# Linear attention, one core: shared wait registers, a warm-up of nine wide matmuls, and VectorE's first head in another order

## The chip, the cores and the metric

The kernel runs on one core of a Trainium2 chip. The metric is the device time of one execution in microseconds (us). TensorE (PE) multiplies, VectorE (DVE), ScalarE (ACT) and GpSimd (POOL) do the elementwise work, SyncE (SP) issues the transfers.

## The reference

For each of 32 heads, q, k and v are 2048 x 128 in bf16:

```python
phi_q = jnp.where(q > 0, q + 1, jnp.exp(q)) + 1e-6
phi_k = jnp.where(k > 0, k + 1, jnp.exp(k)) + 1e-6
kv = jnp.einsum("bhsd,bhse->bhde", phi_k, v)
z = jnp.einsum("bhsd->bhd", phi_k)
num = jnp.einsum("bhqd,bhde->bhqe", phi_q, kv)
den = jnp.einsum("bhqd,bhd->bhq", phi_q, z)[..., None] + 1e-6
return num / den
```

Inputs are 50.3 MB, the output is 16.8 MB.

## The kernel before

phi(x) is computed as min(exp(x), 1) + 1e-6 plus max(x, 0), and the two summands are kept apart: for k they are `emk_sb` and `rk_sb`, for q `emq_sb` and `rq_sb`. A product with phi is then two matmuls into the same PSUM place.

One head goes through these steps. SP loads k, v and q (L371 to L373, 512 KB each) into one of six buffers each. ACT takes exp of k (`ek_sb`, L376). POOL takes max(k, 0) (`rk_sb`, L379; for head 1 DVE does it), DVE min(exp, 1) + 1e-6 (`emk_sb`, L382). For five of the sixteen tiles of 128 rows (`ADD`) POOL adds the two (L387). PE transposes q in two halves of eight tiles (L415, into `xT_ps`) and builds kv (L397) and, where no column of ones beside v does it, z with a one-column matmul (L330, the helper `mm_held`, which uses the weights that are loaded already). ACT and DVE copy kv and z out (`kvs_sb`, L406, L408). ACT takes exp of the transposed q (L426); relu of q is done by DVE for the first half (L435) and by ACT for the second (L433), for heads 0 and 1 by DVE for both. DVE makes `emq_sb` (L447). PE multiplies phi(q) with kv and z (L463, L464, into `o_ps`: five banks of three tiles, the sixteenth tile shared between the first two), DVE adds 1e-6 to the denominators, takes reciprocals and multiplies (L485, L491, L496, L503), and SP stores 512 KB (L549).

The order on each engine is written out by hand: every operation is added to a `Plan` with a key, and the operations of an engine are issued in the order of their keys. `place` (L350) overrides keys for the first heads. `Plan.emit` works out which semaphore values each operation has to wait for, and leaves out waits that earlier ones imply.

PE's stream of heads 1 to 30 is a hardware loop of five turns of six heads (`run_loop`, L165). Since a semaphore's awaited value grows from turn to turn, it stands in a register. Each semaphore x has a register of its own, set by `reg_mov` just ahead of the loop (L180); each wait is followed by a `reg_add` to the next awaited value (L188, L189):

```python
eng.wait_ge(sem_of(x), reg[x])
eng.reg_add(reg[x], reg[x], (l[i + 1] if i + 1 < len(l) else l[0] + step[x]) - v)
```

Ahead of head 0 PE runs a warm-up on zeros (`warm`, L340): 42 matmuls of 125 columns, the first with a load of weights (L344), the others through `mm_held`. They write columns of three `o_ps` banks that no result uses.

PE's order around the start is: warm-up, transposes of head 0, kv of head 0, the register moves, and the loop with transposes and kv of head 1, numerators of head 0, transposes and kv of head 2, and so on. The transposes of head 1 overwrite `xT_ps` and wait, half by half, for exp and relu of head 0; kv of head 1 waits for the copies of head 0 (L406, L408).

DVE's order for the first head is: emk of head 0, relu of the first half, rk of head 1, relu of the second half, emq of head 0, z of head 0, emk of head 1.

SP's order of loads at the start is k, q, v of head 0, k, q, v of head 1, k and q of head 2, k of head 3, v of head 2, and so on. Stores come late: the store of head h has the key h + 1 + 0.18 h, so that loads go ahead of them and a line of stores is left at the end.

Of the kernel before, what the change touches and what calls it, by code (L numbers as in the profile page):

```python
# [12 lines left out]
def _ap(base: bass.AP, elem_offset: int, dims):  # L13
    return bass.AP(base.tensor, base.offset + elem_offset, [list(base.ap[0])] + [list(d) for d in dims])
# [6 lines left out]
class Plan:  # L21
# [3 lines left out]

    def __init__(self):
        self.ops = []
        self.writer = {}
        self.readers = {}

# [31 lines left out]
    def emit(self, nc, block, sems, dma_sem, loop):  # L62
        order = self.order()
# [4 lines left out]
        ops = order["pe"]  # L68
        l0, l1 = (next(x for x in range(len(ops)) if ops[x].tag == t) for t in loop[:2])
        n = (l1 - l0) // loop[2]  # L70
# [26 lines left out]
        at = {e: 0 for e in order}  # L97
        left = sum(len(l) for l in order.values())
        waits = {}
        while left:  # L100
            moved = False
            for e, ops in order.items():
                while at[e] < len(ops):
                    op = ops[at[e]]
# [3 lines left out]
                    k = known[e]  # L108
# [22 lines left out]
        def sem_of(s):  # L131
            return dma_sem(s[1:]) if s[0] == "dma" else sems[s[0]]

        def emit_op(e, eng, op):
            last = op.emit(eng)
            if op.dma:
                last.then_inc(dma_sem(op.dma), 16)
            elif op.sem is not None:
                last.then_inc(sems[op.kind], 1)

        def turns_of(ops, l0, n, turns):
            body = []
            for i in range(n):
                same = [ops[l0 + t * n + i] for t in range(turns)]
                assert len({o.sem is None for o in same}) == 1
                asked = [dict(waits[id(o)]) for o in same]
                for t, o in enumerate(same):
                    for s in {s for a in asked for s in a}:
                        full = max([d.val for d in o.deps if d.sem == s and not (d.eng == "pe")], default=None)
                        if full is not None:  # L150
                            asked[t][s] = full
                for s in asked[1]:
                    if s not in asked[0]:
                        asked[0][s] = 2 * asked[1][s] - asked[2][s]
                        assert 0 < asked[0][s] <= ops[l0 - 1].clock.get(s, 0), (s, asked)
                assert len({tuple(sorted(a)) for a in asked}) == 1, asked
                row = []
                for s in asked[0]:
                    steps = {asked[t + 1][s] - asked[t][s] for t in range(turns - 1)}
                    assert len(steps) == 1, (s, asked)  # L160
                    row.append((s, asked[0][s], steps.pop()))
                body.append((same[0], row))
            return body

        def run_loop(e, eng, l0, n, turns):  # L165
            body = turns_of(order[e], l0, n, turns)
            seq, step, plan = {}, {}, []
            for _, row in body:
                for x, v, d in row:
                    assert step.setdefault(x, d) == d  # L170
                    seq.setdefault(x, []).append(v)
            for x, l in seq.items():
                before = max(l) - step[x]
                if 0 < before and order[e][l0 - 1].clock.get(x, 0) < before:
                    eng.wait_ge(sem_of(x), before)
                seq[x] = sorted({v for v in l if v > before})
            reg = {}
            for k, (x, l) in enumerate(seq.items()):
                reg[x] = eng.alloc_register(f"turn_{k}")
                eng.reg_mov(reg[x], l[0])  # L180
            at = {x: 0 for x in seq}
            with nc.Fori(0, turns, engines=OrderedEngineSet([eng.engine])):
                for op, row in body:
                    for x, v, _ in row:
                        l, i = seq[x], at[x]
                        if i < len(l) and v >= l[i]:
                            assert v == l[i]
                            eng.wait_ge(sem_of(x), reg[x])  # L188
                            eng.reg_add(reg[x], reg[x], (l[i + 1] if i + 1 < len(l) else l[0] + step[x]) - v)  # L189
                            at[x] = i + 1  # L190
                    emit_op(e, eng, op)
            assert all(at[x] == len(l) for x, l in seq.items())

        def run(e, eng):
            ops, i = order[e], 0
            while i < len(ops):
                if e == "pe" and ops[i].tag == loop[0]:
                    l1 = next(x for x in range(len(ops)) if ops[x].tag == loop[1])
                    turns = loop[2]
                    assert (l1 - i) % turns == 0  # L200
                    run_loop(e, eng, i, (l1 - i) // turns, turns)
                    i = l1
                    continue
                op = ops[i]
                for s, v in waits[id(op)]:
                    eng.wait_ge(sem_of(s), v)
                emit_op(e, eng, op)
                i += 1
            if e == "sp":
                for name, n in counts.items():  # L210
                    if name[0] == "o":
                        eng.wait_ge(dma_sem(name), 16 * n)

        if "pool" in order:
            @block.gpsimd
            def _(g):
                run("pool", g)
        if "sp" in order:
            @block.sync
            def _(g):  # L220
                run("sp", g)
        if "act" in order:
            @block.scalar
            def _(g):
                run("act", g)
# [10 lines left out]
def bass_standalone__linear_attn_elu__prompt_kernel(  # L236
# [14 lines left out]
    NC = D + 1  # L251
# [16 lines left out]
    with ExitStack() as es:  # L268
# [22 lines left out]
        o_ps = es.enter_context(nc.psum_tensor("o_ps", [P, NB * 512], fp32))  # L291
# [13 lines left out]
        pl = Plan()  # L305
# [11 lines left out]
        zero_sb = o_sb[:, NBO - 1, 0, :]  # L317
# [11 lines left out]
        def mm_held(pe, out_ap, rhs, stop, start=False):  # L329
            return pe.add_instruction(mybir.InstMatmult(  # L330
                start_tensor_calc=start, stop_tensor_calc=stop, ldweights=False, bass_skip_group_check=True,
                tile_position=(0, 0), tile_size=(P, P), name=nc.get_next_instruction_name(), engine=mybir.EngineType.PE,
                ins=[pe.lower_ap(rhs), pe.lower_ap(held[0])], outs=[pe.lower_ap(out_ap)]))

        held = [None]
        WARM = 42

        def warm(pe):
            held[0] = zero_sb
            for w in range(WARM):  # L340
                b = 2 + w % 3
                o_ap = o_ps[:, b * 512 + 3 * NC: b * 512 + 3 * NC + 125]
                if w == 0:
                    pe.matmul(o_ap, lhsT=zero_sb, rhs=zero_sb[:, 0:125], start=True, stop=True)  # L344
                else:
                    last = mm_held(pe, o_ap, zero_sb[:, 0:125], True, True)
            return last
        pl.add("pe", -9, warm, reads=[("warm",)], writes=[("banko", 2), ("banko", 3), ("banko", 4)])

        place = {("ek", 1): -1.05, ("ek", 2): -0.05, ("ek", 3): 0.1,  # L350
                 ("emk", 0): -2.05, ("rk", 1): -1.95, ("emq", 0): -1.85, ("zs", 0): -1.75, ("emk", 1): -1.7, ("emq", 1): -0.051,
                 ("zs", LAST): LAST - 1 + 0.902, ("kvs", LAST): LAST - 1 + 0.72}
        halves = {}

# [2 lines left out]
        for h in range(NH):  # L357
            def at(name, key, h=h):
                return place.get((name, h), h + key)
# [70 lines left out]
            def relu_q(part, key, eng, kind, h=h, b3=b3):  # L430
                c = (slice(0, HALF), slice(HALF, 2 * HALF))[part]
                if eng == "act":
                    f = lambda a: a.activation(rq_sb[:, b3, c], xT_ps[:, c], ACT.Relu)  # L433
                else:
                    f = lambda d: d.tensor_scalar(rq_sb[:, b3, c], xT_ps[:, c], 0.0, None, op0=ALU.max)  # L435
                halves[2 + part] = pl.add(eng, key, f, reads=both[part:part + 1] + ([("rq", 1, 1)] if h == 2 and part else []),
                                          writes=[("rq", b3, part)], kind=kind)
# [4 lines left out]
            else:  # L442
                exp_q(2, h - 1.1, "eq")
            relu_q(0, -2.0 if h == 0 else h - 2 + 0.948, "dve", "rq")
            relu_q(1, h - 1.0 if h > 1 else (-1.9, -0.0515)[h], "act" if h > 1 else "dve", "relu")
            pl.add("dve", at("emq", -2 + 0.955),
                   lambda d, b2=b2, b3=b3: d.tensor_scalar(emq_sb[:, b3, :], eq_sb[:, b2, :], 1.0, EPS, op0=ALU.min, op1=ALU.add),  # L447
                   reads=[("eq", b2, 0), ("eq", b2, 1)], writes=[("emq", b3)], kind="emq")
# [140 lines left out]
```

## Time and profile before

| | us |
|---|---|
| median of three runs | 171.12 |
| range of the runs | 170.94 to 172.7 |
| the profiled execution, its own time | 170.23 |
| its span, first to last instruction | 168.4 |
| PE busy | 158.5 (94%) |
| ACT, DVE, POOL busy | 155.6, 151.8, 103.5 |
| moved by DMA | 67.26 MB, mean 400 GB/s |
| granted TensorE clock, mean | 0.998 |

The profile is of one execution, whose own time is 170.23; the span leaves out 1.8 us around it. Busy times of engines overlap. "PEld" is the loading of weights, which runs beside PE's matmuls. "Idle before" a group of instructions is put down to what released it; "issue" means that the engine waited for nothing that the profile shows. Register instructions are run by an engine's sequencer and are not counted as busy.

### The profile page before, as it was taken

To read this page: it belongs to the slowest core of one execution; us is meant where nothing else is said; L and a number is where in the kernel's file an instruction comes from. 1 tells how busy PE (TensorE), PEld (TensorE's weight loads), DVE (VectorE), ACT (ScalarE), POOL (GpSimd) and SP (SyncE) were. 2 spreads that over 40 slices of the span, in tenths; PEclk is the share of its full clock that TensorE was granted. 3 is DMA by queue.
4 is the path that set the end of the run, shared out by engine and by line. 5 is a ranking of instruction groups with operands and counts; after the bars stand their busy time and mean duration, and the time that the engine had idled before them with its cause. 6 is when DMAs were issued, how large, how long until landed. Compare 5 with 4: busy or idle time off the path is not lost.

```text
span 168.4 us, 6771 instructions
## 1 busy us (share of the span) xinstructions
PE 158.5 (94%) x3202; PEld 152.7 (91%) x2465; DVE 151.8 (90%) x298; ACT 155.6 (92%) x143; POOL 103.5 (61%) x71
## 2 busy tenths in 40 slices
PE   7769999799999999999999999999999999999980
PEld 0558999799999999999999999999999999999970
DVE  0457999979999999999999999999999999999973
ACT  3959999979999999999999999999999999999582
POOL 2745677663677666666776656667776666677300
PEclk9999999999999999999999999999999999999999
DMA  5999999999999999999999999999999999999946
GB/s 200 411 419 414 419 407 419 378 400 415 415 413 416 420 419 419 419 418 415 416 419 418 419 419 418 416 419 419 419 419 419 418 415 419 419 419 419 382 185 253
DMA packets 19870, 67.26 MB, mean 400 GB/s; under 512 B 2066, under 2 KB 2194, under 8 KB 19858
## 3 DMA queue, kind: packets, MB, share of 16 engines
q1 hardware_dynamic: 19856, 67.12, 98.8%
q8 instruction: 6, 0.10, 0.2%
q14 instruction: 6, 0.05, 0.1%
q10 hardware_dynamic: 2, 0.00, 0.0%
HBM read 50.33 MB, written 16.78 MB: 399 GB/s over the span
## 4 chain that ended last, share of the span: by engine, by line
PE 86%; DMA 7%; SPq 2%; DVE 2%; issue 1%; DVEq 0%
PE kvz_ps L397 36%; PE o_ps L463 17%; PE o_ps L464 17%; PE xT_ps L415 15%; DMA v_sb<-in_v_dram 7%; SPq L369 2%; DVE o_sb L503 1%; PE kvz_ps L330 1%; DVE rden_sb L491 0%; DVE den_sb L485 0%; DVE o_sb L496 0%; DVEq L268 0%
## 5 line engine op out<-in xcount | busy, mean ns | idle before, releaser
L387 POOL TENSOR_TENSOR rk_sb<-rk_sb,emk_sb 128x640 bf16<-128x640 bf16 x32 | 44.7, 1396 | 51.7 <-DVE emq_sb L447 46.2
L397 PE MATMUL kvz_ps<-v_sb,rk_sb 128*128 128x128 bf16 (+1 forms) x512 | 69.1, 217 | 0.9 <-issue 0.9
L503 DVE TENSOR_TENSOR o_sb<-o_ps,rden_sb 128x768 bf16<-128x768 f32 (+2 forms) x62 | 67.8, 1134 | 0.0
L426 ACT ACTIVATE eq_sb<-xT_ps 128x2048 bf16<-128x2048 bf16 (+1 forms) x33 | 60.1, 1825 | 5.7 <-PE xT_ps L415 4.5
L376 ACT ACTIVATE ek_sb<-k_sb 128x2048 bf16<-128x2048 bf16 x32 | 61.5, 1921 | 1.6 <-DMA k_sb<-in_k_dram 1.6
L463 PE MATMUL o_ps<-kvs_sb,emq_sb 128*128 128x129 bf16 (+1 forms) x536 | 61.1, 217 | 0.2 <-DVE o_sb L496 0.2
L464 PE MATMUL o_ps<-kvs_sb,rq_sb 128*128 128x129 bf16 (+1 forms) x536 | 61.1, 217 | 0.0
L379 POOL TENSOR_SCALAR rk_sb<-k_sb 128x2048 bf16<-128x2048 bf16 x31 | 58.7, 1893 | 2.3 <-DMA k_sb<-in_k_dram 2.3
L330 PE MATMUL kvz_ps<-ones_sb,rk_sb 128*128 128x1 bf16 x428 | 59.6, 165 | 0.0
L397 PE MATMUL kvz_ps<-v_sb,emk_sb 128*128 128x128 bf16 (+1 forms) x352 | 56.9, 218 | 1.1 <-DMA v_sb<-in_v_dram 0.6
L463 PEld LDWEIGHTS o_ps<-kvs_sb,emq_sb 128*128 128x128 bf16 x536 | 50.6, 98 | 0.5 <-DVE o_sb L496 0.4
L464 PEld LDWEIGHTS o_ps<-kvs_sb,rq_sb 128*128 128x128 bf16 x536 | 50.1, 97 | 0.0
L397 PEld LDWEIGHTS kvz_ps<-v_sb,rk_sb 128*128 128x128 bf16 x512 | 46.7, 96 | 2.2 <-issue 1.1
L330 PE MATMUL kvz_ps<-ones_sb,emk_sb 128*128 128x1 bf16 x268 | 44.0, 165 | 0.0
L415 PE MATMUL xT_ps<-ident,q_sb 128*128 128x128 bf16 x512 | 33.8, 219 | 2.1 <-issue 1.6
L415 PEld LDWEIGHTS xT_ps<-ident,q_sb 128*128 128x128 bf16 x512 | 29.9, 98 | 5.9 <-DMA q_sb<-in_q_dram 4.2
L397 PEld LDWEIGHTS kvz_ps<-v_sb,emk_sb 128*128 128x128 bf16 x352 | 33.8, 96 | 1.4 <-issue 1.4
L433 ACT ACTIVATE rq_sb<-xT_ps 128x1024 bf16<-128x1024 bf16 x30 | 30.6, 1019 | 0.0
L435 DVE TENSOR_SCALAR rq_sb<-xT_ps 128x1024 bf16<-128x1024 bf16 x34 | 23.4, 691 | 3.7 <-ACT eq_sb L426 3.4
L382 DVE TENSOR_SCALAR emk_sb<-ek_sb 128x2048 bf16<-128x2048 bf16 x32 | 21.9, 684 | 5.1 <-ACT ek_sb L376 5.1
L447 DVE TENSOR_SCALAR emq_sb<-eq_sb 128x2048 bf16<-128x2048 bf16 x32 | 21.9, 686 | 0.0
L496 DVE TENSOR_TENSOR o_sb<-o_ps,rden_sb 128x128 bf16<-128x128 f32 x31 | 9.0, 291 | 1.1 <-DVE rden_sb L491 0.2
(28 smaller groups left out, 47.6 us busy)
## 6 DMA issues: line engine op xcount, KB each, us to landing
k_sb<-in_k_dram SPq DMA_DIRECT2D x32, 512.0 KB, 14.7
q_sb<-in_q_dram SPq DMA_DIRECT2D x32, 512.0 KB, 14.1
v_sb<-in_v_dram SPq DMA_DIRECT2D x32, 512.0 KB, 14.3
out_dram<-o_sb SPq DMA_DIRECT2D x31, 512.0 KB, 14.8
out_dram<-o_sb SPq DMA_DIRECT2D x1, 288.0 KB, 2.2
out_dram<-o_sb SPq DMA_DIRECT2D x1, 224.0 KB, 2.1
first_sb<-in_v_dram ACTq DMA_DIRECT2D x1, 0.1 KB
```

What stands on the lines that cost most here:

```text
L330: return pe.add_instruction(mybir.InstMatmult(start_tensor_calc=start, stop_tensor_calc=stop, ldweights=False, bass_skip_group_check=True, ...
L376: lambda a, bi=bi, b2=b2: a.activation(ek_sb[:, b2, :], k_sb[:, bi, :], ACT.Exp),
L379: lambda e, bi=bi, b3=b3: e.tensor_scalar(rk_sb[:, b3, :], k_sb[:, bi, :], BIG, 0.0, op0=ALU.min, op1=ALU.max),
L387: pl.add("pool", h + 0.5, lambda g, added=added: g.tensor_tensor(out=added(rk_sb), in0=added(rk_sb), in1=added(emk_sb), op=ALU.add), reads ...
L397: last = pe.matmul(kvz_ps[:, 1 - l:NC + r], lhsT=w, rhs=v_sb[:, bi, c - l:c + D + r], start=first, stop=fin, skip_group_check=True)
L415: last = pe.transpose(xT_ps[:, j * P:(j + 1) * P], q_sb[:, bi, j * P:(j + 1) * P], ident[:])
L426: halves[part] = pl.add("act", key, lambda a: a.activation(eq_sb[:, b2, c], xT_ps[:, c], ACT.Exp), reads=both[part:part + 1] or both, writ ...
L433: f = lambda a: a.activation(rq_sb[:, b3, c], xT_ps[:, c], ACT.Relu)
L435: f = lambda d: d.tensor_scalar(rq_sb[:, b3, c], xT_ps[:, c], 0.0, None, op0=ALU.max)
L463: pe.matmul(o_ap, lhsT=emq_sb[:, b3, t * P:(t + 1) * P], rhs=kvs_sb[:, b3, c0:c1], start=True, stop=False)
L464: return pe.matmul(o_ap, lhsT=rq_sb[:, b3, t * P:(t + 1) * P], rhs=kvs_sb[:, b3, c0:c1], start=False, stop=True)
L503: pl.add("dve", key, lambda d: d.tensor_tensor(out=o_sb[:, bo, 3 * g0:3 * g1, :].rearrange("p (a b) d -> p a b d", b=3), in0=_ap(full, bas ...
```

## The change

Three things change.

1. `run_loop` is split. `set_up` works out the waits, and gives a register to each pair of step and value instead of each semaphore: semaphores that are awaited at the same value with the same step share it. A register is raised once a turn, at the last wait that uses it, so the loop has 9 register adds a turn instead of 56 (and one for its count in both). The moves that set the registers are 9 instead of 21, and are issued by the warm-up (`moves`), ahead of the transposes of head 0, not ahead of the loop; the move for the loop's count stays there. Waits that no longer have an add to sit on stand on the matmul that follows, or as 12 instructions of their own.
2. The warm-up has nine matmuls of 500 columns instead of 42 of 125.
3. DVE's order for the first head is: emk of head 0, relu of the first half, relu of the second half, emq of head 0, rk of head 1, emk of head 1, z of head 0.

PE's built stream, a matmul that loads its weights counted as two, has 1463 instructions instead of 1543; the loop has 1077 instead of 1112.

```diff
-        def run_loop(e, eng, l0, n, turns):
+        def set_up(e, eng, l0, n, turns):
             body = turns_of(order[e], l0, n, turns)
-            seq, step, plan = {}, {}, []
+            most, step, entry, now = {}, {}, [], {}
             for _, row in body:
                 for x, v, d in row:
                     assert step.setdefault(x, d) == d
-                    seq.setdefault(x, []).append(v)
-            for x, l in seq.items():
-                before = max(l) - step[x]
-                if 0 < before and order[e][l0 - 1].clock.get(x, 0) < before:
-                    eng.wait_ge(sem_of(x), before)
-                seq[x] = sorted({v for v in l if v > before})
+                    most[x] = max(v, most.get(x, 0))
+            for x, v in most.items():
+                now[x] = v - step[x]
+                if 0 < now[x] and order[e][l0 - 1].clock.get(x, 0) < now[x]:
+                    entry.append((x, now[x]))
+            asks, ends = [], {}
+            for i, (_, row) in enumerate(body):
+                ask = []
+                for x, v, d in row:
+                    if v > now[x]:
+                        now[x] = v
+                        ask.append((x, (d, v)))
+                        ends[(d, v)] = i
+                asks.append(ask)
             reg = {}
-            for k, (x, l) in enumerate(seq.items()):
-                reg[x] = eng.alloc_register(f"turn_{k}")
-                eng.reg_mov(reg[x], l[0])
-            at = {x: 0 for x in seq}
+            for k, (d, v) in enumerate(ends):
+                assert v > 0
+                reg[(d, v)] = eng.alloc_register(f"turn_{k}")
+                self.moves.append(lambda r=reg[(d, v)], v=v: eng.reg_mov(r, v))
+            return body, asks, ends, entry, reg
+
+        def run_loop(e, eng, turns, ready):
+            body, asks, ends, entry, reg = ready
+            for x, v in entry:
+                eng.wait_ge(sem_of(x), v)
             with nc.Fori(0, turns, engines=OrderedEngineSet([eng.engine])):
-                for op, row in body:
-                    for x, v, _ in row:
-                        l, i = seq[x], at[x]
-                        if i < len(l) and v >= l[i]:
-                            assert v == l[i]
-                            eng.wait_ge(sem_of(x), reg[x])
-                            eng.reg_add(reg[x], reg[x], (l[i + 1] if i + 1 < len(l) else l[0] + step[x]) - v)
-                            at[x] = i + 1
+                for i, (op, _) in enumerate(body):
+                    for x, key in asks[i]:
+                        eng.wait_ge(sem_of(x), reg[key])
+                    for key, l in ends.items():
+                        if l == i:
+                            eng.reg_add(reg[key], reg[key], key[0])
                     emit_op(e, eng, op)
...
-        WARM = 42
+        WARM = 9
 
         def warm(pe):
             held[0] = zero_sb
+            zeros = _ap(zero_sb, 0, [[0, 4], [1, 125]])
             for w in range(WARM):
                 b = 2 + w % 3
-                o_ap = o_ps[:, b * 512 + 3 * NC: b * 512 + 3 * NC + 125]
+                o_ap = o_ps[:, b * 512:b * 512 + 500].rearrange("p (a b) -> p a b", b=125)
                 if w == 0:
-                    pe.matmul(o_ap, lhsT=zero_sb, rhs=zero_sb[:, 0:125], start=True, stop=True)
+                    pe.matmul(o_ap, lhsT=zero_sb, rhs=zeros, start=True, stop=True)
                 else:
-                    last = mm_held(pe, o_ap, zero_sb[:, 0:125], True, True)
+                    last = mm_held(pe, o_ap, zeros, True, True)
+            while pl.moves:
+                pl.moves.pop(0)()
             return last
...
         place = {("ek", 1): -1.05, ("ek", 2): -0.05, ("ek", 3): 0.1,
-                 ("emk", 0): -2.05, ("rk", 1): -1.95, ("emq", 0): -1.85, ("zs", 0): -1.75, ("emk", 1): -1.7, ("emq", 1): -0.051,
+                 ("emk", 0): -2.05, ("rk", 1): -1.92, ("emq", 0): -1.93, ("emk", 1): -1.9, ("zs", 0): -1.75, ("emq", 1): -0.051,
...
-            relu_q(1, h - 1.0 if h > 1 else (-1.9, -0.0515)[h], "act" if h > 1 else "dve", "relu")
+            relu_q(1, h - 1.0 if h > 1 else (-1.95, -0.0515)[h], "act" if h > 1 else "dve", "relu")
```

## The prediction

> **What bounds the kernel now.** I read the page first (busy shares, chain), then who waited for whom on PE, then the chain in order of time, the transfers by window, and last the single events in the trace. All times of the working are us from the start of the profiled execution's span.
>
> ```profile
> span 168.4 us, 6771 instructions
> PE 158.5 (94%) x3202; PEld 152.7 (91%) x2465; DVE 151.8 (90%) x298; ACT 155.6 (92%) x143; POOL 103.5 (61%) x71
> PE 86%; DMA 7%; SPq 2%; DVE 2%; issue 1%; DVEq 0%
> ```
>
> PE carries 86% of the chain that ended last. Its holes are few; the view of waits on PE names them:
>
> ```profile
> PE xT_ps L415 <- issue: 1.6, 1, 1.6
> PE kvz_ps L397 <- issue: 0.9, 1, 0.9
> PE kvz_ps L397 <- DMA v_sb<-in_v_dram: 0.6, 1, 0.6
> ```
>
> "issue" means that PE waited for nothing that the profile shows. The chain in order of time says which of the three count:
>
> ```profile
> 5.10 11.86 DMA v_sb<-in_v_dram
> 16.97 0.21 issue
> ...
> 31.79 0.94 issue
> ```
>
> The 1.6 (before the first transposes of the loop, at 10.67) is not in the chain: PE must wait for head 2's v anyway, which lands at 16.97. From 17.18 on PE never pauses, except for the 0.94 at 31.79. In the window 32.8 to 160 it is busy all the time, but so are the DMA engines:
>
> ```profile
> 17.20:31.60 14.40, 14.40 (x297) 14.30 (x232) 13.84 (x27) 14.16 (x13) 9.41 (x7) 1.00 1.03 415
> 31.60:32.80 1.20, 0.26 (x6) 0.08 (x3) 1.20 (x3) 1.20 (x2) 1.20 (x2) 1.00 1.09 406
> 32.80:160.00 127.20, 127.20 (x2623) 126.22 (x2039) 123.99 (x236) 123.17 (x105) 84.25 (x52) 1.00 1.02 415
> ```
>
> Columns: PE, PEld, DVE, ACT, POOL busy, granted clock, DMA share, GB/s. A DMA share of 1.02 over 127 us leaves no free transfer time there. At the end it falls off (transfers from 152 to 168.4, 0.41 us a number):
>
> ```profile
> GB/s 420 420 420 420 410 430 410 410 440 400 410 410 410 440 390 410 460 350 210 190 230 410 400 350 140 150 40 20 30 20 90 400 430 390 304 382 379 214 0 0
> ```
>
> The 20 to 40 GB/s about 163 are one engine's rate (418 over 16 is 26): one DMA engine still works when the others are done. The sixteen completions of each store show it too: of head 29's store fifteen have landed by 163.2 and the last at 165.33; of head 28's, by 161.96 and at 164.04. That engine finishes 162.70, 164.04, 165.33, 166.57, 167.34, 167.89 (the end) back to back, while the fifteen others finish the last piece at 167.71 to 167.86. It loses some 0.12 a store on the others over the whole run. So two bounds end within 0.1 of each other: PE's chain and this engine.
>
> **The change, part by part.**
>
> *Warm-up (before L344, after L359).* The 42 matmuls run from 1.02 to 4.77; the first 26 stand 105 ns apart, the rest 52. Nine of 500 columns are four such each: 0.42 slow, 0.21 fast. With the same switch at 3.73 they end at 1.02 + 2.71 + 2.55 x 0.21 = 4.27, all slow at 4.80. Both are before q of head 0 lands (5.31; first transpose 5.35). Saved: 0. If the clock fell back, head 0's transposes and kv (0.85 + 2.08) would double, +2.9 at 9.0; the loop's earlier start (1.5, below) and the wait for v (0.85 from transposes to kv) cover 2.3 of it, so 0 to 0.6 lost; I take 0, since the clock held over today's pause of 0.58. The Trainium skill's "TensorE: Matmul & The Clock Gate" (The HAM clock gate) has the warm-up as some 3.4 us of time, not a count; by that the switch would be at 4.4 and the warm-up would end near 4.7, still ahead of q. The trace switched after 2.7.
>
> *Registers before the loop.*
>
> ```profile
> L180 PEldq MOVE  x21: 29/29/29, 8.4 to 10.2; - x21
> L189 PEldq ALU_OP  x280: 32/32/42, 10.4 to 155.0; - x140
> ```
>
> 22 moves, 0.09 from one to the next, fill 8.40 to 10.36 on PE's sequencer (21 of L180 and one for the loop's count): that is the 1.6. Now nine moves (0.8) follow the nine warm-up matmuls and are over before 4; one, for the loop's count, stays. Transposes of head 1 can then follow kv of head 0 (ends 9.0) and q of head 1 (lands 9.11): 9.2 instead of 10.67.
>
> *VectorE's order.* Now relu's second half, emq, rk of head 1, emk of head 1, zs. With the row starts of today (0.60 a step, rk 0.83): relu 8.02, emq 8.62, rk 9.22, emk 10.05 to 10.7, zs to 10.9. The second relu half comes 0.8 earlier and frees the transposes' bank; ACT's exp of q moves from 11.76 to some 10.3. zs now stands behind emk (which waits for ACT's exp of k, done 9.80); PE's kv of head 1 waits for it, so kv starts at 10.95, against 11.56. Add on POOL follows emk at 10.8 (10.91 today). What is late next: kv of head 2, which waits for v at 16.97. SP's loads up to it were issued by 5.10 and wait for nothing that moves. So of 0.6 and 1.5 gained here nothing passes; one or two register adds behind that wait (0.09 each) go: 0.1.
>
> *Waits in the loop.* 56 register adds a turn become 9, twelve waits stand alone. 47 x 0.09 = 4.2 of sequencer time a turn is hidden: the sequencer runs up to 1 us ahead, and matmuls follow each other at 55 to 58 ns across the adds. One turn of six heads takes 28.77; the matmuls alone at 55.6 and 27 ns make 28.6. So 0 to 0.2 a turn, 0 to 0.9 in all; I take 0, as the spacings beside the adds equal those away from them.
>
> *The hole at 31.79.* No wait stands there: it lies between kv's first matmul and the next weight load. PE's queue q8 brought instructions just before:
>
> ```profile
> q8 instruction: 1, 0.02, 4.5%
> ```
>
> (window 30 to 31.5; its packet ran 30.22 to 31.30.) Six packets make 0.10 MB for 1543 instructions: 64 B each, 256 a packet. Counting in the built stream puts the hole at instruction 963, and other ends of blocks at 195, 451, 707, 1219. Blocks were fetched at 14.81, 21.93, 30.22, 36.73 and 43.35, 4.0 to 5.8 after the sequencer entered the one before, and could be used 1.43 after the packet's end (at 32.73, and at 39.10, where an add comes 0.56 late but PE's queue covers it). From entering to use: 6.4, 6.5, 6.6, 6.6 and once 8.3, which is the hole: 31.57 to 32.73, 1.11 more than a step. After: the stream has 1463, the loop starts at 136 instead of 181, so the same boundaries fall elsewhere: 195 in kv of head 1 (sequencer at 11.4), 451 in the numerators of head 1, 707 in the transposes of head 4, 963 at the numerators of head 4, and 1219 behind the loop. With kv of head 2 at 17.1 and today's 4.82 and 4.72 a head, PE needs 451 at 20.0, 707 at 26.8, 963 at 33.6; the sequencer is 1 us ahead there and enters 451 near 18.7 and 707 near 25.8. Adding 6.4 to 8.3 to the entry before: 451 is ready 17.8 to 19.7, 707 25.1 to 27.0, 963 32.2 to 34.1. Margins of 1.4 to 2 at 6.4; at 8.3 a hole of 0.2 to 0.5. I take the hole as gone, -1.1; ends -1.1 and, at two slow fetches, -0.3.
>
> The Trainium skill's "Runtime: NRT & Kernel Launch" (Instruction fetch mechanics) has blocks of 256 instructions, the crossing mostly hidden, and a stall at a taken branch out of the window. By it the loop's branch back would cost; the trace has none (heads 6 to 7 take 4.82 like others), but one crossing that was not hidden.
>
> *The sum.* PE's path: 0.1 + 1.1 = 1.2 earlier. The last store: the fifteen engines follow, to 166.6. The late engine has its whole queue from long before (its store of head 28 was issued at 154.98 and landed 164.04), so it goes on to 167.9. End of span: 168.4 less 0 to 1.2; by the late engine, 0.1. Its own time is 170.23, so 170.1. The median of the runs, 171.12, is 0.89 above that execution. Either that stays (171.0), or it is more of the same holes, and goes (170.1); I take the middle, **170.6**.
>
> **Rivals.**
> 1. Forecast: late engine holds the end, 170.1 to 171.0. For: its back-to-back landings. Chance 0.50.
> 2. The whole 1.2 passes (the late engine is not late in other executions, or is hit by fewer fetches): 169.9, and with the 0.89 as low as 169.0. For: the chain ends on DVE and PE. Against: 167.89. Chance 0.25.
> 3. Slower: an instruction fetch lands on the late engine. Each fetch takes 0.9 to 1.1 of one engine; the lags of the sixteen completions step up by 1.1 to 1.6 after each. The last block (at 162.45 today, when DMA is free) is now fetched on leaving the loop, near 160, when it is not. On the late engine it would cost 0.9 to 1.1: 172.0 to 172.2. It decides if that fetch starts before 162 and on that engine. Chance 0.12.
> 4. The hole comes back elsewhere (a fetch over 8 us): the change doesn't do what it says, 171.1. Chance 0.13.
>
> **How the numbers follow.** Forecast 170.6 as the likeliest. Range 169.5 (rival 2 with half of the 0.89) to 172.0 (rival 3's low end); outside, a third of rival 2 and most of rival 3. About 1% (1.7 us) is what a measurement of this kernel can tell from no change: faster than 169.4 takes rival 2 with most of the 0.89, 0.09; slower than 172.8 takes rival 3 with a bad run, 0.06; within, 0.85.
>
> **What would show it.** Right: no "issue" of 1.6 before the transposes of head 1 (start near 9.2), kv of head 2 still at 17.1, no hole on PE up to 160, PE's end near 162.5, and the last completion still near 167.9, one engine behind fifteen. Wrong: the last store lands at 166.7 (rival 2); a gap of over 0.5 between matmuls in the first turn (rival 4); transposes 105 ns apart in head 0 (clock fell); a last landing past 168.5 with the fifteen others before 167 (rival 3).

## The result, and the profile after

The changed kernel takes 170.01 us (median of 22 runs, 169.57 to 171.1), the kernel before 170.71 (22 runs beside them, 169.92 to 172.7). The ratio is 0.9963, 95% interval 0.9947 to 0.998: 0.4% faster, within the 1% that was called no change. The forecast was 170.6, 0.3% under the median of three runs (171.12) that was known then. The two profiled executions took 170.23 and 169.75 themselves.

The page of the changed kernel, its span, busy times and the engines of the chain:

```profile
span 168.0 us, 6551 instructions
PE 159.1 (95%) x3169; PEld 153.3 (91%) x2465; DVE 151.9 (90%) x298; ACT 155.6 (93%) x143; POOL 103.5 (62%) x71
q8 instruction: 5, 0.08, 0.2%
PE 89%; DMA 4%; DVE 2%; ACT 1%; SPq 1%; issue 0%; DVEq 0%
```

"issue" has left the chain, and PE's instructions now come in five packets. The waits on PE (engine and line, for whom, us in all, times, longest):

```profile
PE kvz_ps L414 <- DMA v_sb<-in_v_dram: 1.1, 1, 1.1
PE o_ps L359 <- DVE o_sb L333: 1.0, 1, 1.0
PE kvz_ps L414 <- DVE kvs_sb L425: 0.5, 1, 0.5
PE xT_ps L432 <- DMA q_sb<-in_q_dram: 0.4, 1, 0.4
PE o_ps L480 <- DVE o_sb L513: 0.2, 1, 0.2
```

Neither the "issue" wait of 1.6 before the loop nor that of 0.9 in the first turn (the hole: a pause of PE behind no wait) is left. The windows about the old hole (PE, PEld, DVE, ACT, POOL busy, clock, DMA share, GB/s) show PE busy right through it:

```profile
17.20:31.60 14.40, 14.40 (x301) 14.29 (x234) 14.20 (x28) 14.34 (x14) 9.88 (x7) 1.00 1.03 414
31.60:32.80 1.20, 1.20 (x32) 1.19 (x19) 1.20 (x2) 1.20 (x1) 1.20 (x2) 1.00 1.04 420
32.80:158.50 125.70, 125.70 (x2592) 124.78 (x2020) 123.63 (x236) 122.72 (x105) 83.96 (x52) 1.00 1.03 418
```

PE's last matmul starts at 162.16, against 163.65: 1.49 earlier. The span ends only 0.4 earlier. Transfers from 152 to 168.4, 0.41 us a number, show where the rest is:

```profile
GB/s 390 450 410 400 460 380 420 420 390 430 410 410 450 390 440 400 390 400 420 420 370 270 250 160 90 50 40 320 430 390 306 406 369 350 27 27 13 0 0 0
```

After 350 there stand 27, 27 and 13: for 1.1 us one DMA engine alone still writes. In the row before the change 20 to 40 stood at 163, ahead of the last stores; now it stands behind them. The semaphore events say the same. Each of these stores shows sixteen completions, read here as one from each DMA engine; of those of the last piece fifteen have come at 166.39 and the last at 167.49; before, at 167.86 and 167.89. SP, which waits for the last completion, waits 1.4 us in the kernel before (first line) and 2.5 in the changed one (second):

```profile
SPq L212 <- DMA out_dram<-o_sb: 1.4, 1, 1.4
SPq L226 <- DMA out_dram<-o_sb: 2.5, 1, 2.5
```

### The profile page after: what moved, and what is told of

Read it like the earlier page. It is cut to its first block, busy times and chain, and to the rows that moved or that the text cites. A ratio compares the mean times of both kernels' runs of the same rounds, so it can differ in the third digit from the quotient of the medians.

```text
span 168.0 us, 6551 instructions
## 1 busy us (share of the span) xinstructions
PE 159.1 (95%) x3169; PEld 153.3 (91%) x2465; DVE 151.9 (90%) x298; ACT 155.6 (93%) x143; POOL 103.5 (62%) x71
## 4 chain that ended last, share of the span: by engine, by line
PE 89%; DMA 4%; DVE 2%; ACT 1%; SPq 1%; issue 0%; DVEq 0%
PE kvz_ps L414 37%; PE o_ps L480 18%; PE o_ps L481 17%; PE xT_ps L432 16%; DMA k_sb<-in_k_dram 4%; DVE o_sb L520 1%; PE kvz_ps L344 1%; ACT ek_sb L393 1%; SPq L386 1%; DVE emk_sb L399 0%; DVE rden_sb L508 0%; DVE den_sb L502 0%; DVE o_sb L513 0%; DVEq L282 0%; DVE kvs_sb L425 0%
## 5 line engine op out<-in xcount | busy, mean ns | idle before, releaser
L432 PE MATMUL xT_ps<-ident,q_sb 128*128 128x128 bf16 x512 | 34.5, 222 | 0.4 <-DMA q_sb<-in_q_dram 0.4
L432 PEld LDWEIGHTS xT_ps<-ident,q_sb 128*128 128x128 bf16 x512 | 30.6, 99 | 4.4 <-DMA q_sb<-in_q_dram 4.4
L399 DVE TENSOR_SCALAR emk_sb<-ek_sb 128x2048 bf16<-128x2048 bf16 x32 | 21.9, 684 | 6.0 <-ACT ek_sb L393 6.0
L464 DVE TENSOR_SCALAR emq_sb<-eq_sb 128x2048 bf16<-128x2048 bf16 x32 | 22.4, 699 | 0.0
```

The source lines that it names most:

```text
L432: last = pe.transpose(xT_ps[:, j * P:(j + 1) * P], q_sb[:, bi, j * P:(j + 1) * P], ident[:])
```

## The experiments

Theory A: the kernel before had two bounds that end together, PE's chain (with a hole where a block of PE's instructions came late) and one DMA engine that is behind the fifteen others; the change removes the hole, and the late engine takes back much of the gain. Rivals: the gain comes from the fewer register instructions themselves, or from VectorE's order; or the end simply follows PE; or it follows the bytes that DMA moves.

Columns: start of kv of head 2; the pause at the old hole's place; start of PE's last matmul; the fifteenth and the sixteenth completion of the last store (all from one profiled execution, us); then the median and the ratio to the kernel before as it ran beside each (medians 170.64 to 170.71).

| kernel | kv 2 | hole | last matmul | 15th | 16th | median | ratio (95%) |
|---|---|---|---|---|---|---|---|
| before | 17.18 | 1.17 | 163.65 | 167.86 | 167.89 | 170.71 | 1 |
| changed | 16.87 | none | 162.16 | 166.39 | 167.49 | 170.01 | 0.9963 (0.9947 to 0.998) |
| e1 registers alone | 18.03 | none | 163.42 | 167.64 | 167.69 | 170.22 | 0.9973 (0.9951 to 0.9996) |
| e2 warm-up alone | 17.41 | none | 162.94 | 167.17 | 167.75 | 170.31 | 0.9987 (0.9967 to 1.0008) |
| e3 order alone | 17.08 | 1.10 | 163.78 | 167.98 | 168.00 | 170.79 | 1.001 (0.9988 to 1.0033) |
| e4 changed, 11 wide | 17.25 | none | 162.54 | 166.77 | 167.54 | 169.77 | 0.9943 (0.9922 to 0.9963) |
| e5 changed, 3 stores split | 17.84 | none | 163.14 | 167.96 | 167.97 | 170.8 | 1.0005 (0.9982 to 1.0028) |
| e6 before, 3 stores split | 16.70 | 1.15 | 163.30 | 167.54 | 168.19 | 170.74 | 1.0009 (0.9993 to 1.0025) |
| e7 as e4, 3 stores split | 16.50 | none | 161.79 | 167.99 | 168.04 | 170.45 | 0.9993 (0.9978 to 1.0008) |
| e8 before, a store left out | 17.45 | 1.15 | 164.03 | 168.23 | 168.25 | 170.54 | 0.9991 (0.9969 to 1.0013) |
| e9 changed, a store left out | 17.79 | none | 163.09 | 167.27 | 167.30 | 169.18 | 0.9916 (0.9882 to 0.9949) |
| e10 as e4, 2 stores in three | 17.32 | none | 162.62 | 168.78 | 169.39 | 171.43 | 1.0036 (1.0008 to 1.0064) |
| e11 as e4, again | 16.95 | none | 162.25 | 166.47 | 167.74 | 169.88 | 0.9957 (0.993 to 0.9983) |
| e12 changed, again | 17.48 | none | 162.78 | 167.01 | 168.22 | 170.28 | 0.9965 (0.9936 to 0.9994) |

Two things in the table bear on every row. From the start of kv of head 2 to the last matmul PE takes 145.3 in the eight kernels with the whole new stream, 145.4 in e1, 145.5 in e2 (it has a pause of 0.28 at 22.2) and 146.5 to 146.7 in the four with the old stream: on this stretch the whole change is worth 1.2 to 1.4 each time. But where the stretch starts varies by more than that, from 16.50 to 18.03, so PE's end in a single execution does not show the gain.

**e1, the registers alone.** The changed kernel with the old warm-up and VectorE's old order (main lines):

```diff
-        WARM = 9
+        WARM = 42
...
-                 ("emk", 0): -2.05, ("rk", 1): -1.92, ("emq", 0): -1.93, ("emk", 1): -1.9, ("zs", 0): -1.75, ("emq", 1): -0.051,
+                 ("emk", 0): -2.05, ("rk", 1): -1.95, ("emq", 0): -1.85, ("zs", 0): -1.75, ("emk", 1): -1.7, ("emq", 1): -0.051,
```

> The new registers and moves alone: the old warm-up of 42 matmuls and VectorE's old order are kept. Theory A (two bounds: a hole on PE from a late block of instructions, and one late DMA engine that holds the last landing): the loop starts at instruction 169 instead of 181, the block ends fall elsewhere, and the hole of 1.1 goes; PE ends 1.2 to 1.5 us earlier, fifteen DMA engines land the last piece that much earlier, the sixteenth only 0 to 0.5; time 0.3 to 0.7 us below before, ratio 0.996 to 0.998. Theory B (the end follows PE): ratio 0.991 to 0.993. Theory C (the registers do nothing, the gain is of the warm-up or of VectorE's order): ratio 1.000.

The hole is gone and the ratio as expected. In the profiled execution PE did not gain 1.2: kv of head 0 waited 2.0 us for v, the clock fell during that pause (0.54 of full speed in 9 to 12), kv of head 1 started at 13.2, and kv of head 2 at 18.03, 0.9 later than before. The hole's 1.1 paid for that.

**e2, the warm-up alone.** The kernel before, with only the warm-up changed (main lines):

```diff
-        WARM = 42
+        WARM = 9
...
-                    last = mm_held(pe, o_ap, zero_sb[:, 0:125], True, True)
+                    last = mm_held(pe, o_ap, zeros, True, True)
```

> The nine wide matmuls alone; old registers and old order. Theory A: the stream loses 33 instructions ahead of the loop, so the block ends fall elsewhere (963 in kv of head 4, needed about 32.8, ready 31.4 to 33.3): the hole shrinks to under 0.5 or goes, although not one wait has changed; ratio 0.996 to 0.998. The 1.6 us before the transposes of head 1 stays. Theory B, that the saved adds and moves make the gain: ratio 1.000, hole of about 1 us still there.

No wait, register or operation of the loop differs, only 33 instructions ahead of it. Of PE's two "issue" waits, the one before the loop stays and the one in the first turn is gone:

```profile
PE xT_ps L416 <- issue: 1.2, 1, 1.2
PE o_ps L345 <- DVE o_sb L319: 1.0, 1, 1.0
PE kvz_ps L398 <- DMA v_sb<-in_v_dram: 1.0, 1, 1.0
PE xT_ps L416 <- DMA q_sb<-in_q_dram: 0.3, 1, 0.3
PE o_ps L464 <- DVE o_sb L497: 0.2, 1, 0.2
```

So the saved adds are not needed to remove the hole: it goes when the ends of the blocks fall elsewhere. The fetch was as late as in the kernel before (its packet ran from 30.68 to 31.74), but PE comes to the block's end only near 33.0, in the middle of kv of head 5 (the expectation has head 4). The first matmul behind that end started at 33.00, 1.27 after the packet's end, so the 1.43 that the prediction took from two places is not fixed. The ratio of 0.9987 lies above the 0.996 to 0.998 expected and can't be told from 1: that removing the hole by itself shortens the time is not shown.

**e3, the order alone.** The kernel before with VectorE's new keys:

```diff
-                 ("emk", 0): -2.05, ("rk", 1): -1.95, ("emq", 0): -1.85, ("zs", 0): -1.75, ("emk", 1): -1.7, ("emq", 1): -0.051,
+                 ("emk", 0): -2.05, ("rk", 1): -1.92, ("emq", 0): -1.93, ("emk", 1): -1.9, ("zs", 0): -1.75, ("emq", 1): -0.051,
...
-            relu_q(1, h - 1.0 if h > 1 else (-1.9, -0.0515)[h], "act" if h > 1 else "dve", "relu")
+            relu_q(1, h - 1.0 if h > 1 else (-1.95, -0.0515)[h], "act" if h > 1 else "dve", "relu")
```

> VectorE's new order alone; stream of PE as before, instruction for instruction. Theory A: transposes of head 1 still start near 10.7, kv of head 2 still at 17.1, the block ends are where they were, and a hole of about 1 us stands at instruction 963 if that fetch is slow again; ratio 1.000, at most 0.999. Theory B, that the order carries the gain: ratio 0.996.

```profile
PE xT_ps L415 <- issue: 1.2, 1, 1.2
PE o_ps L344 <- DVE o_sb L319: 1.0, 1, 1.0
PE kvz_ps L397 <- issue: 0.9, 1, 0.9
```

Both "issue" waits are there, the hole at the same place. In all four kernels with the old stream of instructions (before, e3, e6, e8) it is there, 1.10 to 1.17 long; in the ten others it is in none.

**e4, a longer warm-up.** The changed kernel with eleven wide matmuls:

```diff
-        WARM = 9
+        WARM = 11
```

> The changed kernel with eleven wide matmuls instead of nine. In its trace the clock was not granted until 6.8 and the transposes of head 0 ran at 107 ns. Theory A: the first head is covered by the wait for v of head 2 (16.7 to 17.0), and the end by the late DMA engine, so no difference from the changed kernel: ratio to before 0.996. Theory B: the slow clock costs up to 0.9 us; with a longer warm-up the transposes run at 56 ns and the ratio falls to 0.991 to 0.993.

Theory B's reading of the clock did not hold: the switch came at 7.03, so the transposes of head 0 ran slow here as well, and what a fast first head is worth stays untested by this run. The end came where the late engine put it, 167.54. The ratio, 0.9943, is below the changed kernel's 0.9963; e11 and e12 take this up.

**e5 to e7, work moved between DMA engines.** Three stores in the line at the end (heads 21, 23, 25) are issued in two parts (main lines; the second part has a semaphore of its own): in the changed kernel (e5), in the kernel before (e6) and in e4's kernel (e7).

```diff
...
-            if h < LAST:
+            if h in (21, 23, 25):
+                store(0, NT, late, ("t", 0, 1, 2, 3, 4), bo, 0, 120)
+                store(0, NT, late + 0.001, ("t", 0, 1, 2, 3, 4), bo, 120, P, "op")
+            elif h < LAST:
                 store(0, NT, late, ("t", 0, 1, 2, 3, 4), bo)
```

> The changed kernel, with the stores of heads 21, 23 and 25 (in the line of stores at the end) each issued as 120 rows and then 8 rows. The same bytes are stored. Theory A (one late DMA engine holds the end): if the 120 rows pass that engine by, it is relieved of three times 1.38 us and its lag of some 4.2 us at 160 is gone; the last landing then follows the fifteen others, 1.1 us earlier than in the trace of the changed kernel: time 168.8 to 169.2, ratio 0.989 to 0.992. The Trainium skill, 'DMA: Bandwidth & Descriptors' (how many engines), has a transfer use the largest number of engines up to 16 that divides its rows; by that 120 rows use fifteen, and which one is left out is not known from the traces. If the late engine is not the one left out, its lag stays or grows by 0.2 to 0.5, ratio 0.996 to 0.999. Theory B (the end follows PE's chain and no DMA engine): ratio 0.996 as the changed kernel.

> The kernel before with the same three stores split. Theory A: PE's chain ends it within 0.1 us of the late engine (fifteen engines land at 167.86, the sixteenth at 167.89), so relieving that engine alone gains at most 0.1: ratio 1.000. Together with e5 it tells whether both bounds are there: split alone 0, change alone 0.4%, both 1.0%. Theory B: a line of split stores is simply faster: the same gain here as in e5 over the changed kernel.

> The changed kernel with eleven wide matmuls and the three split stores. Theory A: the late engine is gone as a bound, so what the warm-up does to PE's start now shows: in its trace kv of head 2 started at 17.25 and in the changed kernel's at 16.87, so within 0.4 us of e5; ratio 0.988 to 0.992. Theory B: ratio 0.994 as without the split.

The late engine is not the one that the 120 rows leave out: one engine now runs ahead of the others, and the late one gets a row more a store, from the 8. So the second branch of the e5 text holds by its cause: the last landing moves from 167.49 to 167.97 (e5) and from 167.54 to 168.04 (e7); e5's ratio, 1.0005, lies just above that branch's numbers. Three rows of 4 KB are 0.47 at the engine's 1.25 us for eight. e7 is the sharpest: PE ends 0.75 earlier than in e4, the earliest of all, and the kernel is slower, 0.9993 against 0.9943. Its transfers from 152 to 168, 0.4 us a number:

```profile
GB/s 410 379 369 399 379 369 369 358 399 338 369 338 410 369 430 389 307 399 399 399 389 369 287 256 225 215 164 410 420 399 330 386 218 252 371 92 71 45 45 4
```

The trickle behind the last store is two engines now (45). e6 measured 1.0009, within the error of 1, as expected, though its last landing moved by 0.3. The gain that e5 and e7 were meant to bring did not come, and e7's 0.9993 fits neither theory's numbers, since the split put more work on the late engine; what they show is the late engine's hold on the end.

**e8 and e9, one store less.** The store of head 12 is left out, of the kernel before (e8) and of the changed kernel (e9):

```diff
-            if h < LAST:
+            if h == 12:
+                pass
+            elif h < LAST:
```

> The kernel before without the store of head 12 (its output is left out). One store less is 1.25 us less for every DMA engine and 1.38 for the late one. Theory A: PE's chain of the kernel before ends at 167.9 by itself, so the span stays within 0.2; ratio 0.998 to 1.000. Theory B (the kernel is bound by the bytes that the DMA engines move, whose share is 1.02 over 127 us): 1.25 us less, ratio 0.992 to 0.993.

> The changed kernel without the store of head 12 (its output is left out). In its trace fifteen DMA engines land the last piece at 166.39, the late one at 167.49. Theory A (the late engine holds the end of the changed kernel): it is relieved of 1.38 us and lands with the others; the span falls by 0.8 to 1.1 us, ratio to before 0.989 to 0.992, where the same store left out of the kernel before gave 0.9991. Theory B (the end follows PE): ratio 0.996, as with the store.

Before: 0.9991, no gain, though 0.5 MB less was moved; fifteen engines land at 168.23, the late one at 168.25, as PE set it. Changed: 0.9916 against 0.9963 with the store, 0.8 us; against e12, the changed kernel run beside it, 1.1 us (169.18 and 170.28). The late engine has caught up: the trickle behind the last store is gone (changed kernel without the store, 152 to 168):

```profile
GB/s 389 451 379 461 389 420 410 430 420 379 440 399 430 399 369 287 225 195 92 164 389 430 379 103 20 20 31 10 0 0 328 410 410 296 386 385 372 36 0 0
```

20 to 31 stand about 162 again, ahead of the last stores. The profiled execution of e9 started kv of head 2 late, at 17.79, so PE set its end, and its last landing (167.30) is only 0.2 earlier than with the store; the times of the runs carry the reading. This pair excludes both rivals: an end that follows PE alone would leave e9 at 0.996, above its interval, and one that follows the bytes would give e8 0.7%, below its interval.

**e10, to find the late engine.** In e4's kernel two stores are issued in three parts (main lines):

```diff
...
-                store(0, NT, late, ("t", 0, 1, 2, 3, 4), bo)
+                store(0, NT, late, ("t", 0, 1, 2, 3, 4), bo, 0, 64)
+                store(0, NT, late + 0.001, ("t", 0, 1, 2, 3, 4), bo, 64, 113, "op")
+                store(0, NT, late + 0.002, ("t", 0, 1, 2, 3, 4), bo, 113, P, "oq")
```

(The three lines are for heads 21 and 25; the other heads keep the one line.)

> The changed kernel with eleven wide matmuls; the stores of heads 21 and 25 are issued as 64, 49 and 15 rows. By the Trainium skill, 'DMA: Bandwidth & Descriptors' (how many engines), the 49 rows use seven engines. e5 showed the late engine among the eight that took its 8 rows. Theory A, it is the eighth of them: six rows less for it, 0.9 us, eight rows more for the first seven, 1.25 us; the last landing comes 0.4 to 0.6 us earlier, ratio 0.990 to 0.993. Theory B, it is one of the seven: the last landing comes 1.2 us later, ratio 1.000 to 1.003.

Theory B held: the last landing moves to 169.39, 1.65 to 1.85 later than in e4 and e11, with PE where it was; the ratio, 1.0036, lies just above that theory's numbers. So the late engine is one of the seven that took the 49 rows. No other engine fits: before the split stores the next one was 1.2 us less late (2.65 against 3.88 behind the first), and with 1.25 more it would, by an estimate from these lags, have ended near 167.5. By the Trainium skill, "DMA: Bandwidth & Descriptors" (how many engines), such a transfer takes the lowest-numbered engines, here the first seven; the trace has no engine numbers to show that. The extra eight rows account for 1.25; the cause of the rest is open.

**e11 and e12, the longer warm-up and the changed kernel side by side.** No edit but `WARM`, which is 11 in e11.

> The changed kernel with eleven wide matmuls once more, beside the changed kernel on one chip. Theory A (the late engine holds both, the warm-up only keeps the clock in the executions that lose it): ratio 0.994 to 0.996 and 0 to 0.3 us below the changed kernel. Theory B (the earlier gain was chance): same as the changed kernel.

> The changed kernel once more, on the same chip: ratio 0.995 to 0.998 by either theory; executions with a mean granted clock under 0.98 some 0.7 us above the rest.

169.88 and 170.28, 0.40 apart where at most 0.3 was expected; the intervals, 0.993 to 0.9983 and 0.9936 to 0.9994, overlap almost wholly. Twice the longer warm-up had the lower median, but no difference is shown. In the changed kernel's first 22 runs the three whose mean granted clock was under 0.98 took 170.74, 170.93 and 171.1, the slowest; in e12 one at 0.979 took 169.83, against the expectation, so the clock alone does not decide.

## Why the prediction was right, point by point

The end is the later of two: PE's last matmul plus 4.2 us, and the late engine. In the ten rows of the table without split stores, and in e6, the fifteenth completion is 4.18 to 4.24 behind PE's last matmul, whatever the kernel. The late engine landed the last piece at 167.49 to 168.22 wherever it came last by over 0.4 without extra rows; the 167.89 of the kernel before lies among these. That is the forecast's mechanism, a chain of PE freed of its hole and one engine that holds the end.

The number owes more to luck. Of the forecast gain of 0.52 only 0.1 came from that mechanism; 0.42 was half of a gap that three runs had left. The measured 170.01 lies 0.1 below the band of the likeliest case (170.1 to 171.0) and 0.1 above that of rival 2 (169.0 to 169.9): the time alone would not have told them apart, the landings do.

- **Warm-up, 0.** Right in its price. Its working was not: the switch of the clock was taken at 3.73, with 4.80 for the end if all nine were slow; they were all slow, and the clock came only at 6.8, near the end of head 0's transposes (107 ns apart, the sign that the prediction gave for a clock that fell). It cost nothing here because kv of head 0 waited for v, which landed at 7.94.
- **Registers and VectorE's order, 0 beyond 0.1.** Right. The moves ran at 1.0 to 1.8, while the warm-up's matmuls, queued ahead of them, still ran. The transposes of head 1 started at 10.45, not 9.2: k and q of head 1 landed 1.3 later in this execution (9.18, 10.40), which hid what the moves gave. e3 shows nothing for the order (1.001, 0.9988 to 1.0033).
- **The wait for v of head 2.** kv of head 2 was forecast at 17.1 and started at 16.87: v landed at 16.72 instead of 16.97, and PE followed 0.15 behind instead of 0.21. So this term was 0.3, not 0.1; the same kernel started it at 17.48 in e12, so this is one draw. The prediction took the wait for v as fixed, and overlooked what it waits for: before, fifteen completions of v of head 2 had come by 15.45 and the last at 16.97, with the first block of PE's instructions fetched from 14.81. In the eight traces where that fetch began between 14.73 and 15.60 the last completion of this v came 0.8 to 2.2 behind the fifteenth, in the five where it began at 15.62 or later at most 0.23 behind. (In e1, fetched at 14.10, two came together, 0.8 behind the rest.) That the fetch delays one engine's share of v is read from this order; no run moves the fetch alone.
- **Adds in the loop, 0.** Right: six heads take 28.77 to 28.78 in both kernels, but for 28.83 in the one turn before that has the pause at 99.8.
- **The hole, 1.1.** Right, in place, size and reason; e2 shows that 33 instructions fewer are enough. The last block was fetched at 157.77 (forecast "near 160").
- **PE's sum, 1.2.** Measured 1.49: 1.12 of the hole, 0.31 at kv of head 2, and a pause of 0.06 at 99.8 that the changed kernel does not have.
- **The late engine, 167.9.** It landed at 167.49, so 0.4 passed in this pair of executions, not 0.1. In e12, the same kernel, it landed at 168.22: the 0.4 lies within the spread from one execution to the next and is not shown to be the change's.
- **The median.** The 0.89 between the profiled execution and the median of three runs was split in the middle. With 22 runs the median before is 170.71, only 0.48 above that execution; 0.41 of the 0.89 was three runs' chance. The forecast gain of 0.52 met the measured 0.70 partly by that. Where the 0.70 comes from is only in part shown: an execution that PE ends, as in e3 and e8, gains from the lost hole, one that the late engine ends does not, and how many of each there are was not measured.

Rival 2 (the whole 1.2 passes) fell with the landings, though not by the time; rival 4 (the hole moves) did not come. Rival 3 came half true: the last block was fetched before 162 with the DMA engines still full, but not on the late engine, whose landings of whole stores keep their spacing of 1.27 to 1.41.

## What to carry to other kernels

When the chain names PE and the DMA share is 1.02 as well, look at the last sixteen completions one by one before pricing a gain on PE: here 1.5 us on PE became 0.4 at the end of the profiled executions and 0.70 in the medians, since one engine of sixteen, invisible in the mean share, had its own queue to finish. The pause in the loop's first turn that had no wait and was gone in later turns was here a late block of instructions, and an edit ahead of the loop that shifted the stream by 33 instructions (e2) removed it; so look at where the blocks end before judging a change of instruction count by its own cost. Leaving one transfer out, of both kernels, told a bound of PE from a bound of DMA here in two runs. And one profile is one draw: kv of head 2 started anywhere within 1.5 us, more than the gain, so compare stretches between two fixed points and the medians.

## What the runs showed of the hardware that was not expected

- Each fetch of 16 KB of PE's instructions while the data queue was full put one DMA engine 1.1 to 1.6 us behind until the queue emptied near 162, a different one each time: in the kernel before, the sorted lags of the sixteen completions step up after 14.8, 21.9, 30.2, 36.7 and 43.4. The late engine of the end is another one, which lost some 0.12 to 0.15 at every store (in the kernel before its lag grows from 3.43 to 4.52 over eight stores between 150 and 160); why it does so is open.
- A transfer of 120 rows left one engine out: its completion came at once and that engine then ran ahead of the others, by 2.0 us in e7, 3.1 in e5 and 3.6 in e6 near 158.6. The Trainium skill, "DMA: Bandwidth & Descriptors" (how many engines), has that as the largest number up to 16 that divides the rows; the trace agrees.
- The clock's switch moved far: full speed came from 3.69 (e12) to 7.03 (e4) with PE started at 1.02 each time, and in e1, e5 and e9 it fell back in the first head after pauses of 1.4 to 2.2 us and returned at 11.3 to 12.5. In these three the clock's records stand 3.41 us apart (in e1 granted at 4.91, cut at 8.32, granted at 11.74). Pauses of 1.4 to 1.7 in the kernel before, e8 and e12 left it at full speed, so the length of a pause alone does not decide. The Trainium skill, "TensorE: Matmul & The Clock Gate" (The HAM clock gate), calls the warm-up run-variable; these spreads bear that out.
